# Weight blocks loaded and decoded in pairs, with other waits and ranks in the plan

## The chip, the core and the metric

The kernel runs on one core of one Trainium2 chip. The core has a matrix engine (PE in the profile), a vector engine (DVE), a scalar engine (ACT), a general engine (POOL) and SP, which here only issues transfers to the core's 16 DMA engines. Each engine works through its own instructions in the order in which they were written out, and waits for others by semaphores. The metric is the device time of one execution in microseconds (us), the median of several runs. Lower is better.

## What is computed

Causal attention with a decay bias over 8 batches of 8 heads, 576 positions and head size 64, and behind it a feed-forward layer of 4608 tokens, width 512 and inner width 2048. The weights of the second part come as 64-bit floats.

```python
scores = scale * np.matmul(q, k.transpose(0, 1, 3, 2))
cum = np.cumsum(np.maximum(s, 0.0), axis=-1)
bias = -(cum[:, :, :, None] - cum[:, :, None, :])
scores = np.where(causal, -1000000000.0, scores + np.minimum(bias, 0.0))
attn = np.exp(scores - np.max(scores, axis=-1, keepdims=True))
attn = attn / (np.sum(attn, axis=-1, keepdims=True) + 1e-09)
x = np.matmul(attn, v)            # then tokens x 512
h = x @ w_in                      # 512 -> 2048
g = np.where(h > 0.0, h, np.exp(np.minimum(h, 0.0)) - 1.0)
out = g @ w_out                   # 2048 -> 512
```

## The kernel before

**A plan.** The code does not issue instructions in the order in which it is written. Every piece of work is an operation with a priority, the ways in which it can be done (an engine and an estimated cost for each), and what it reads and writes. `Plan.issue` then picks, again and again, the operation with the smallest rank: the time at which it could start by the plan's estimates, and among those that could start at the same time the smaller priority number. It so writes out one fixed order for each engine. The estimates are nanoseconds; a load costs SP 460 ns and lands when a modelled pipe of 225 bytes per ns has passed its bytes, plus 1800 ns. PE operations that fill gaps (`fillers`, L1547: transposes of an identity that nothing reads) take a rank 350 ns later than their start, and exist only in the first 60 us of planned time.

**Attention.** The first 320 rows of the batches 0 to 2 are done as 12 "low" pairs of heads in 32-bit floats (`prepare_low`, `scoring_low`, `weighing_low`, priorities 0, 10, ... 110). Each pair loads its keys, queries and values, and the row of decay sums: pair (0,1) from the tile `aux` in SBUF, all later ones from the DRAM copy `sums_dram`. `decay_parts` rewrites `aux` in place right after the second pair has been scored. The rest of the attention (`Unit`, priorities from 120) uses 16-bit halves of q, k and v; its operand sets are written to DRAM and read back.

**Feed-forward.** The tokens go in 18 chunks of 256. Chunk 0 is native: it multiplies 32-bit weights (L1423, first layer, into tiles `h`; L1477, second layer, into `o`). The chunks 1 to 17 use weights split in two 16-bit halves, three products for one (L1427 and L1484). Their PE operations have priority 10000 and up: attention goes first where it can start.

**The weights.** `load_unit` handles one block of 128 inner columns (`kind` 0, from w_in) or rows (`kind` 1, from w_out), 128 x 512 values: 32 blocks. Each block is loaded raw (512 KB) into one of four slots of `raws`, and decoded from 64 to 32 bits: one ACT operation (L693), one on DVE or ACT (L697, L699), one on DVE that joins the two into `wa` (L702), and the largest magnitude of the block by DVE (L623) or by ACT (L626, with a second instruction that reads the accumulator). Every load has the sum load of pair (0,1) as a `late` condition: the plan may place it only behind that one's planned landing (`urgent`). When all 32 blocks are there, `weight_scales` finds one scale for each of the two matrices, and `split_unit` splits each block: the high half on POOL, ACT or DVE (L428 to L430), the low half on DVE (L717), with priority -500 + f, ahead of all attention.

**Memory.** `wa` holds 4 tiles of 4 blocks of both kinds (16 KB per partition each), `wp`, the split halves, 4 tiles as large; `raws` shares the first `wp` tile. The values of the first group of units take the place of the last `wp` tile, later ones that of the first `wa` tile; the second operand set takes that of the second `wa` tile, and two of the transposed attention tiles `T` those of the others, once they have been free.

Of the kernel before, what the change touches and what calls it, by code (L numbers as in the profile page):

```python
# [35 lines left out]
LAG, RATE = 1800.0, 225.0  # L36
W0, WD = 25, 3

F_EARLY = 6

W_GROUP = 4

# [5 lines left out]
N_FREE = 0  # L48

N_NATIVE, N_RAW = 1, 4  # L50

FILL_T, GAP = 60e3, 350.0

# [39 lines left out]
class Op:  # L93
    __slots__ = ("ways", "after", "before", "behind", "bufs", "new", "prio", "ready", "left", "filler")


class Plan:
# [97 lines left out]
    def issue(self):  # L195
# [19 lines left out]
        while pending:  # L215
# [11 lines left out]
            for o in pending:  # L227
                t = 0.0
                for b, k in o.new:
# [4 lines left out]
                    if b.others and (b.always or not busy):  # L234
                        for key, bufs, *rule in b.others:
                            if rule and not rule[0](taken[key]):
                                continue
# [6 lines left out]
                else:  # L244
# [9 lines left out]
                    rank = (start + GAP if o.filler else start, o.prio)  # L254
# [4 lines left out]
            if o.filler:  # L259
                start -= GAP  # L260
# [95 lines left out]
def kernel(  # L356
# [223 lines left out]
    NG = NF // W_GROUP  # L580
    w_all = [plan.buf(sb, [P, W_GROUP, 2, 512], F32, f"wa_{g}") for g in range(NG)]
    w_parts = [plan.buf(sb, [P, W_GROUP, 2, 2, 512], F16, f"wp_{g}") for g in range(NG)]

    def weight(f, kind):
        return (w_all[f // W_GROUP], (f, kind)), lambda: w_all[f // W_GROUP].v[:, f % W_GROUP, kind]

    def weight_part(f, kind, part):
        return ((w_parts[f // W_GROUP], (f, kind, part)),
                lambda: w_parts[f // W_GROUP].v[:, f % W_GROUP, kind, part])
# [7 lines left out]
    A_LOW, A_IN, A_OUT = 0, N_LOW * (NP + 1), N_LOW * (NP + 1) + NF + 1  # L597
    A_GROUP = A_OUT + NF + 1
# [38 lines left out]
    def scales_of(prio, spans, dst):  # L637

        n = len(spans)
        kind = int(dst == 0)  # L640
# [25 lines left out]
    def weight_scales():  # L666

        scales_of(-600, [(A_IN, NF + 1), (A_OUT, NF + 1)], 0)
        op(-600, [("DVE-SB", 100.0, lambda: power(
            scales.v.bitcast(U32)[:, 3:4], scales.v.bitcast(U32)[:, 1:2], 2 * 127))],  # L670
           [(scales, 0)], [(scales, 3)])

    urgent = []
    raws = plan.buf(sb, [P, N_RAW, 512, 2], U32, "raws", tag=w_parts[0].key[1])

    def load_unit(f, kind, src):

        prio = W0 + WD * f
        a, n = src.shape[1], f"{'io'[kind]}{f}"
        place, value = weight(f, kind)  # L680
# [972 lines left out]
```

## Time and profile before

| | us |
|---|---|
| median of 3 runs | 1038.81 (1037.28 to 1039.48) |
| the profiled execution | 1034.6 |
| its span, first to last instruction | 1032.8 |
| PE busy | 1003.1 (97%) |
| DVE busy | 845.2 (82%) |
| ACT busy | 669.0 (65%) |
| POOL busy | 295.9 (29%) |

The granted PE clock was 0.996 of full speed over the span. A busy PE counts the fillers too. The view by windows cuts the span into stretches and gives, for each engine, the busy time in it and its number of instructions. The view by lines groups instructions by source line, tile and shape, with the mean time of one in ns and the idle time that the engine had just before them. The timeline lists instructions in order of time, with neighbours of one kind merged; a bracket at the end tells how long the engine sat idle before, and what released it.

### The profile page before, as it was taken

To read this page: it belongs to the slowest core of one execution; us is meant where nothing else is said; L and a number is where in the kernel's file an instruction comes from. 1 tells how busy PE (TensorE), PEld (TensorE's weight loads), DVE (VectorE), ACT (ScalarE), POOL (GpSimd) and SP (SyncE) were. 2 spreads that over 40 slices of the span, in tenths; PEclk is the share of its full clock that TensorE was granted. 3 is DMA by queue.
4 is the path that set the end of the run, shared out by engine and by line. 5 is a ranking of instruction groups with operands and counts; after the bars stand their busy time and mean duration, and the time that the engine had idled before them with its cause. 6 is when DMAs were issued, how large, how long until landed. Compare 5 with 4: busy or idle time off the path is not lost. (4 is left out here: it accounts for less than half of the span.)

```text
span 1032.8 us, 21782 instructions
## 1 busy us (share of the span) xinstructions
PE 1003.1 (97%) x7305; PEld 688.7 (67%) x7305; DVE 845.2 (82%) x2346; ACT 669.0 (65%) x1559; POOL 295.9 (29%) x487
## 2 busy tenths in 40 slices
PE   8889999999999999999999999999999999999998
PEld 6667656676666666666666666676666676666665
DVE  7999998788988988898889999798988898863232
ACT  4898755666667766776776766666675765644343
POOL 6343452242323323241234242222232123100000
PEclk9999999999999999999999999999999999999999
DMA  7997524589979997999989987979998998841000
GB/s 197 276 289 236 150 72 95 124 190 213 222 166 212 207 192 165 198 202 208 196 174 201 232 179 174 229 181 192 215 198 196 227 202 187 182 94 47 1 21 21
DMA packets 296724, 179.83 MB, mean 174 GB/s; under 512 B 209908, under 2 KB 270564, under 8 KB 296612
## 3 DMA queue, kind: packets, MB, share of 16 engines
q1 hardware_dynamic: 296612, 178.45, 75.7%
q8 instruction: 57, 0.93, 0.4%
q14 instruction: 55, 0.45, 0.2%
HBM read 93.08 MB, written 36.81 MB: 126 GB/s over the span
## 5 line engine op out<-in xcount | busy, mean ns | idle before, releaser
L1427 PE MATMUL h<-xh,wp 128*128 128x256 f16 x2176 | 402.7, 273 | 0.7 <-DVE gg L1466 0.7
L1484 PE MATMUL o<-wp,gg 128*128 128x512 f16 x1632 | 392.7, 380 | 0.5 <-DVE gg L1466 0.5
L1427 PEld LDWEIGHTS <-wp 128*128 128x128 f16 x3264 | 317.4, 98 | 69.7 <-issue 2.1
L1427 PE MATMUL h<-xl,wp 128*128 128x256 f16 x1088 | 297.3, 273 | 1.1 <-DVE xl L1403 1.1
L1484 PEld LDWEIGHTS <-gg 128*128 128x128 f16 x1632 | 157.7, 98 | 144.5 <-DVE gg L1466 1.0
L1073 ACT ACTIVATE p<-p,mn 128x192 f32<-128x192 f32 (+1 forms) x232 | 143.7, 620 | 54.9 <-DVE mn L1068 52.9
L1133 DVE SCALAR_TENSOR_TENSOR p<-p,sm,p 128x512 f16<-128x512 f32 (+3 forms) x257 | 162.8, 662 | 4.9 <-POOL p L1125 2.4
L1459 DVE SCALAR_TENSOR_TENSOR h<-g,cs,h 128x512 f32<-128x512 f32 x136 | 102.0, 750 | 60.5 <-ACT g L1446 59.2
L1125 POOL TENSOR_SCALAR p<-p,sm 128x512 f16<-128x512 f32 (+3 forms) x94 | 65.1, 696 | 290.5 <-DVE sm L1079 117.1
L1439 ACT ACTIVATE g<-h,cs 128x512 f32<-128x512 f32 x136 | 92.8, 682 | 78.0 <-PE h L1427 77.2
L1463 ACT ACTIVATE gg<-h 128x512 f16<-128x512 f32 x132 | 78.3, 593 | 83.2 <-DVE h L1459 79.3
L1068 DVE CUSTOM_DVE_ANT_0 p<-sc,maskw 128x192 f32<-128x192 f32 (+1 forms) x232 | 109.5, 481 | 11.9 <-PE sc L1065 8.5
L1065 PE MATMUL sc<-set 128*128 128x288 f16 (+3 forms) x544 | 112.7, 299 | 4.5 <-DVE mn L1068 4.3
L1466 DVE SCALAR_TENSOR_TENSOR gg<-h,gg 128x512 f16<-128x512 f32 x136 | 93.3, 686 | 16.3 <-ACT gg L1463 15.7
L1129 ACT ACTIVATE p<-p,sm 128x512 f16<-128x512 f32 (+3 forms) x139 | 75.1, 557 | 19.0 <-DVE sm L1079 5.5
L1065 PEld LDWEIGHTS <-set 128*128 128x128 f16 x584 | 55.1, 98 | 41.6 <-issue 8.6
L1252 PE MATMUL av<-T,v 128*64 128x256 f16 (+5 forms) x960 | 62.4, 278 | 2.8 <-DMA T<-p 2.8
L1252 PEld LDWEIGHTS <-v 128*64 128x64 f16 x960 | 48.5, 110 | 23.3 <-issue 12.3
L1446 ACT ACTIVATE g<-g 128x512 f32<-128x512 f32 x81 | 50.9, 628 | 1.9
L428 POOL TENSOR_SCALAR v<-va,scales 128x320 f16<-128x320 f32 (+1 forms) x45 | 26.8, 599 | 64.9 <-PE av L1252 58.3
L1073 ACT ACTIVATION_READ_ACCUMULATOR p<-p,mn 128x1 f32 x232 | 43.7, 188 | 0.0
L1068 DVE CUSTOM_DVE_ANT_0 p<-sc,maskw,mn 128x288 f32<-128x288 f32 x64 | 32.9, 514 | 7.1 <-PE sc L1065 5.5
(200 smaller groups left out, 1261.0 us busy)
## 6 DMA issues: line engine op xcount, KB each, us to landing
set<-spread SPq DMA_DIRECT2D x32, 432.0 KB
spread<-parts_None SPq DMA_DIRECT2D x32, 288.0 KB
set<-spread SPq DMA_DIRECT2D x32, 288.0 KB
raws<-in_w_in_dram SPq DMA_DIRECT2D x16, 512.0 KB
raws<-in_w_out_dram SPq DMA_DIRECT2D x16, 512.0 KB
out_dram<-ost SPq DMA_DIRECT2D x32, 256.0 KB
va<-in_vb_dram SPq DMA_DIRECT2D x16, 352.0 KB
xc<-x_dram SPq DMA_DIRECT2D x22, 256.0 KB
```

The costliest lines, as they stand in the source:

```text
L1065: pe_.matmul(view(sc.v[:, :cw]), l, r, start=n == 0, stop=n == len(pairs) - 1)
L1068: op(prio, [("DVE", 84 + dve_p(cw), lambda i=i, sc=sc: dve.tensor_tensor_reduce(pt.v[:, i * cw : (i + 1) * cw], sc.v[:, :cw], mv(i * cw, c ...
L1073: op(prio, [("ACT", 480 + w / 1.2, lambda: act.activation(pt.v[:, :w], pt.v[:, :w], AF.Exp, bias=mn.v[:, n - 1 : n], scale=-1.0, accum_out ...
L1129: ("ACT", 295 + size / 1.2, lambda part=part: act.activation(part(0), own(part), AF.Copy, scale=sm.v[:, r])),
L1133: ("DVE-SB", dve_2(size), lambda part=part: dve.scalar_tensor_tensor(part(1), own(part), sm.v[:, r], part(0), ALU.mult, ALU.subtract)),
L1252: pe_.matmul(av.v[w.h * HB : (w.h + 1) * HB, dst], w.values.v[:, w.h, kb, v], part(w, kb, m), start=kb == 0 and m == 0 and v == 0, stop=kb ...
L1427: pe_.matmul(columns(k), weight_part(f, 0, part)[1]()[:, c * P : (c + 1) * P], xx.v[:, c], start=(c == 0 and m == 0), stop=(c == NCB - 1 a ...
L1439: op(side, [("ACT", act_c(W) + (0 if native else 90), lambda: act.activation(g.v, hp.v, AF.Exp, scale=1.0 if native else by(3)))], [hp] + ...
L1459: op(side, [("DVE", dve_p(W), lambda: dve.scalar_tensor_tensor(hp.v, g.v, by(2 if sign[0] else 1), hp.v, ALU.mult, ALU.max))], [g, cs], [hp])
L1463: ("ACT", act_c(W), lambda: act.activation(gg.v[:, 0], hp.v, AF.Copy, scale=2.0**-DOWN)),
L1466: op(side, [("DVE", dve_p(W), lambda: dve.scalar_tensor_tensor(gg.v[:, 1], hp.v, 2.0**-DOWN, gg.v[:, 0], ALU.mult, ALU.subtract))], [hp, ( ...
L1484: pe_.matmul(acc[i].v, gg.v[:, g, at], weight_part(f, 1, part)[1](), start=(f == 0 and m == 0), stop=(f == NF - 1 and m == 2),)
```

## The change

- The weights are handled in 16 pairs of blocks (128 x 1024 values, 1 MB raw): `load_pair` and `split_pair` in place of `load_unit` and `split_unit`. The raw tiles are four of 1 MB, in the places of the four `wp` tiles of w_out. A pair of w_in is read in rows of 256 columns (2 KB), before 128 (1 KB). The plan counts 5 bytes for a value that has 8.
- The loads of weights have no `late` condition any more. All of batch 0's pairs take their sums from `aux`, and `decay_parts` comes after the fourth pair.
- Each operation has a `gap` that is added to its start in the rank, though not to its start: 400 ns for the weights' loads and decoding, 0 for the splits, 350 for fillers as before. The splits have priority 130 + p.
- The scales of w_in and w_out are found one after the other, and the small operations of a chunk that need only w_in's scale no longer wait for the other's.
- Scores may use the `h` banks until the first `x` tile has been taken, before until the eighth `h`. `wa` and `wp` are tiles of one kind each, and so the tiles that later take their places wait for other blocks: the second operand set for w_in's pairs 3 to 5, the values of later groups for w_in's pairs 0 to 2, two `T` tiles for w_out's pairs 0 to 5.

```diff
-LAG, RATE = 1800.0, 225.0
-W0, WD = 25, 3
-F_EARLY = 6
+LAG, RATE, RAW = 1800.0, 225.0, 5
+W0, WD = 25, 6
+W_PAIRS = 3, 3, 2
-N_FREE = 0
-N_NATIVE, N_RAW = 1, 4
+N_NATIVE, PRIO_SPLIT = 1, 130
+W_GAP, S_GAP = 400.0, 0.0
...
-                    rank = (start + GAP if o.filler else start, o.prio)
+                    rank = (start + o.gap, o.prio)
...
-    w_all = [plan.buf(sb, [P, W_GROUP, 2, 512], F32, f"wa_{g}") for g in range(NG)]
-    w_parts = [plan.buf(sb, [P, W_GROUP, 2, 2, 512], F16, f"wp_{g}") for g in range(NG)]
+    w_all = [plan.buf(sb, [P, n, 2 * 512], F32, f"wa_{kind}_{g}") for kind in range(2) for g, n in enumerate(W_PAIRS)]
+    w_parts = [plan.buf(sb, [P, W_GROUP // 2, 2, 2 * 512], F16, f"wp_{kind}_{g}") for kind in range(2) for g in range(NG)]
...
-    def weight_scales():
-        scales_of(-600, [(A_IN, NF + 1), (A_OUT, NF + 1)], 0)
+    def weight_scales(kind):
+        scales_of(-600, [((A_IN, A_OUT)[kind], NFP + 1)], kind)
...
-    raws = plan.buf(sb, [P, N_RAW, 512, 2], U32, "raws", tag=w_parts[0].key[1])
-    def load_unit(f, kind, src):
-        prio = W0 + WD * f
+    raws = [plan.buf(sb, [P, 2 * 512, 2], U32, f"raw_{g}", tag=w_parts[NG + g].key[1]) for g in range(NG)]
+    def load_pair(p, kind):
+        prio, n = W0 + WD * p, 2 * 512
...
-            slot = (2 * f + kind) % N_RAW
+            slot = raws[(2 * p + kind) % NG]
...
-                 lambda: src.bitcast(U32), [], [(raws, (slot, 0)), (raws, (slot, 1))], P * 4096,
-                 urgent if f >= N_FREE else ())
+                 lambda: src.bitcast(U32), [], [(slot, 0), (slot, 1)], P * n * RAW)
...
-    def split_unit(f, kind):
-        prio, col = -500 + f, slice(kind, kind + 1)
+    def split_pair(p, kind):
+        prio, col = PRIO_SPLIT + p, slice(kind, kind + 1)
...
-            if (b, j) == (0, 1):
-                o = load(prio, lambda: u.k.v[at], lambda: aux.v[h0 : h0 + 2, 0, :LOW],
+            if not b:
+                load(prio, lambda: u.k.v[at], lambda: aux.v[h0 : h0 + 2, 0, :LOW],
...
-            return lambda n: n < last
+            return lambda taken, key: taken[key] < last
...
-                        others=[("h", N_H, opening(1 + N_NATIVE * NFP)), ("o0", 1, opening(1)), ("o1", 1, opening(1))])
+                        others=[("h", N_H, lambda taken, key: not taken[xh.key]), ("o0", 1, opening(1)), ("o1", 1, opening(1))])
...
-                        others=[(w_all[g].key[1], 1, lambda n: n > 0) for g in range(2, NG)], always=True)
+                        others=[(w_all[NW + g].key[1], 1, lambda taken, key: taken[key] > 0) for g in range(2)], always=True)
...
-            if u is todo[1][0]:
+            if u is todo[NP - 1][0]:
                 decay_parts()
...
-        op(side, [("DVE-SB", 600.0, steps)],
-           [(scales, 0), (scales, 3)] + [(scales, c) for c in cols if c > 3], [cs])
+        op(side, [("DVE-SB", 480.0, steps)],
+           [(scales, 0)] + [(scales, c) for c in cols if c > 3], [(cs, "in")])
+        op(side, [("DVE-SB", 120.0, lambda: dve.tensor_scalar(
+            cs.v[:, 4:5], cs.v[:, 3:4], scales.v[:, 3:4], 2.0**DOWN, ALU.mult, ALU.mult))],
+           [(scales, 3), (cs, "in")], [(cs, "out")])
...
-    load_weights(0, F_EARLY)
+    for p in range(NFP):
+        for kind in range(2):
+            plan.gap = W_GAP
+            load_pair(p, kind)
+            plan.gap = 0.0
     xc = load_x(0, chunks[0])
-    load_weights(F_EARLY, NF)
-    weight_scales()
-    for f in range(NF):
-        split_unit(f, 0)
-        split_unit(f, 1)
+    for kind in range(2):
+        weight_scales(kind)
+    for p in range(NFP):
+        for kind in range(2):
+            plan.gap = S_GAP
+            split_pair(p, kind)
+            plan.gap = 0.0
```

More of the change, by code (lines that the diff above doesn't have):

```diff
@@ L93 @@
 class Op:
-    __slots__ = ("ways", "after", "before", "behind", "bufs", "new", "prio", "ready", "left", "filler")
+    __slots__ = ("ways", "after", "before", "behind", "bufs", "new", "prio", "ready", "left", "filler", "gap")
 class Plan:
@@ L235, in issue @@
                         for key, bufs, *rule in b.others:
-                            if rule and not rule[0](taken[key]):
+                            if rule and not rule[0](taken, key):
                                 continue
@@ L258, in issue @@
             (start, _), o, n = best
-            if o.filler:
-                start -= GAP
+            start -= o.gap
             engine, cost, trace = o.ways[n][:3]
@@ L705, in load_unit @@
         else:
             load(prio, lambda: value().rearrange("p (a n) -> p a n", a=a), lambda: src,
-                 [], [place], P * 2048, urgent)
-        peak(prio, 512, value, [place], (A_IN, A_OUT)[kind] + f,
-             aside=(lambda: raw(0).bitcast(F32)) if wide else None, also=[(raws, (slot, 0))] if wide else [])
-    def split_unit(f, kind):
-        prio, col = -500 + f, slice(kind, kind + 1)
-        place, value = weight(f, kind)
-        (high, high_v), (low, low_v) = (weight_part(f, kind, m) for m in range(2))
-        scaled(prio, 512, high_v, value, lambda: scales.v[:, col], [place, (scales, 0)], [high])
-        op(prio, [("DVE-SB", dve_2(512), lambda: dve.scalar_tensor_tensor(
-            low_v(), value(), scales.v[:, col], high_v(), ALU.mult, ALU.subtract))],
-           [place, (scales, 0), high], [low])
@@ L721, in load_weights @@
-    def load_weights(f0, f1):
-        wi = w_in.rearrange("(c p) f -> p c f", p=P)
-        wo = w_out.rearrange("(f p) (a m) -> f p a m", p=P, a=1)
-        for f in range(f0, f1):
-            fs = slice(f * P, (f + 1) * P)
-            load_unit(f, 0, wi[:, :, fs])
-            load_unit(f, 1, wo[f])
+                 [], [place], P * n * 4)
+        peak(prio, n, value, [place], (A_IN, A_OUT)[kind] + p,
+             aside=(lambda: raw(0).bitcast(F32)) if wide else None, also=[(slot, 0)] if wide else [])
@@ new lines, in split_pair @@
+    def split_pair(p, kind):
+        prio, col = PRIO_SPLIT + p, slice(kind, kind + 1)
+        place, value = weight_pair(p, kind)
+        (high, high_v), (low, low_v) = (weight_part(2 * p, kind, m) for m in range(2))
+        scaled(prio, 2 * 512, high_v, value, lambda: scales.v[:, col], [place, (scales, kind)], [high])
+        op(prio, [("DVE-SB", dve_2(2 * 512), lambda: dve.scalar_tensor_tensor(
+            low_v(), value(), scales.v[:, col], high_v(), ALU.mult, ALU.subtract))],
+           [place, (scales, kind), high], [low])
@@ L1042, in prepare @@
              lambda: u.vs.v[:, :1, 0].bitcast(F32), used, [u.vs])
+    xh, xl = (plan.buf(sb, [P, NCB, TMAX], F16, n, tag=n) for n in ("xh", "xl"))
     plan.signal = (id(ps), "o0")
@@ L1332, in attention @@
             step()
-    xh, xl = (plan.buf(sb, [P, NCB, TMAX], F16, n, tag=n) for n in ("xh", "xl"))
     def load_x(ch, rows):
@@ L1517, in output @@
             ]
-            op(side, [w for w in ways if only is None or w[0] in only], reads + [cs], writes)
+            op(side, [w for w in ways if only is None or w[0] in only], reads + [(cs, "out")], writes)
         for i in range(NTB):
```

78 lines of the change are left out of this document (43 added, 35 removed).

## The prediction

> **What bounds the kernel now.** I read the page first, then the view by windows, then the lines, timeline and DMA view of the stretches that the change touches. First the windows: start and end, length, busy time and number of instructions of PE, of the weight loads (PEld), DVE, ACT and POOL, then the granted PE clock, the busy share of the DMA engines and GB/s.
>
> ```profile
> span 1032.8 us, 21782 instructions
> PE 1003.1 (97%) x7305; PEld 688.7 (67%) x7305; DVE 845.2 (82%) x2346; ACT 669.0 (65%) x1559; POOL 295.9 (29%) x487
> ```
> ```profile
> 0.00:20.00 20.00, 14.87 (x92) 13.28 (x92) 14.21 (x33) 8.37 (x27) 14.94 (x38) 0.91 0.65 153
> 20.00:60.00 40.00, 36.69 (x251) 26.41 (x251) 36.08 (x117) 33.44 (x99) 15.49 (x34) 1.00 0.97 291
> 60.00:120.00 60.00, 57.34 (x325) 41.55 (x323) 54.60 (x178) 50.44 (x150) 18.62 (x48) 1.00 0.81 237
> 120.00:150.00 30.00, 29.51 (x110) 18.14 (x110) 29.08 (x77) 17.77 (x35) 16.48 (x17) 1.00 0.24 77
> 150.00:200.00 50.00, 47.48 (x335) 32.46 (x334) 42.91 (x122) 28.65 (x67) 14.69 (x24) 0.97 0.39 93
> 200.00:1000.00 800.00, 788.32 (x6009) 538.20 (x6007) 659.46 (x1810) 519.37 (x1166) 215.68 (x327) 1.00 0.82 179
> ```
> ```profile
> L1547 PE MATMUL scratch<-ident 128*128 128x128 f32 x140 | 19.0, 287 | 0.0
> ```
> ```profile
> L1423 PE MATMUL h<-x,wa x128: 378/380/484, 59.8 to 144.0; 128*128 128x256 f32 x128
> ```
>
> PE is the bound from 60 us on: idle 2.7 us in 60 to 120, 0.5 in 120 to 150, 2.5 in 150 to 200, 11.7 in the next 800. Only the start is different. In the first 60 us PE sits idle 5.1 + 3.3 = 8.4 us, and 19.0 us of its busy time are fillers: 27.4 of 60 us give nothing. This ends where chunk 0's matmuls begin, at 59.8 us; from there PE has spare work. What sets that point is DVE and ACT: in 20 to 60 they are busy 36.1 and 33.4 of 40 us, with the low pairs' softmax and the decoding of weights. So the change is worth what it brings chunk 0's start forward, plus stalls that it removes behind it; PE's own work (1003.1 - 19.0 = 984 us) stays.
>
> **Decoding and splitting, 32 blocks to 16 pairs.** The lines of the stretch from 17 to 119 us, and others that give the price of a width:
>
> ```profile
> L693 ACT ACTIVATE raws<-raws 128x512 f32<-128x512 f32 x32 | 21.6, 678 | 0.6 <-DMA raws<-in_w_in_dram 0.3 <-DMA raws<-in_w_out_dram 0.3
> L626 ACT ACTIVATE raws<-wa 128x512 f32<-128x512 f32 x14 | 9.5, 680 | 1.8 <-DVE wa L702 1.5
> L702 DVE SCALAR_TENSOR_TENSOR wa<-raws 128x512 uint32<-128x512 uint32 x32 | 22.4, 703 | 1.0 <-ACT raws L693 0.3 <-DVE raws L697 0.2
> L697 DVE TENSOR_SCALAR raws<-raws 128x512 uint32<-128x512 uint32 x29 | 13.0, 451 | 0.8 <-DMA raws<-in_w_in_dram 0.8
> L623 DVE TENSOR_REDUCE peaks<-wa 128x1 f32<-128x512 f32 x18 | 12.2, 679 | 0.1
> ```
> ```profile
> L626 ACT ACTIVATION_READ_ACCUMULATOR raws<-wa x14: 178/181/196, 25.2 to 118.9; 128x1 f32 x14
> ```
> ```profile
> L626 ACT ACTIVATE junk<-va 128x704 bf16<-128x704 f32 x4 | 3.2, 789 | 1.5 <-DMA va<-in_vb_dram 1.3
> ```
> ```profile
> L626 ACT ACTIVATE junk<-vs 128x448 bf16<-128x448 f32 x2 | 1.2, 578 | 0.4 <-DMA vs<-in_vb_dram 0.4
> ```
> ```profile
> L623 DVE TENSOR_REDUCE peaks<-vs 128x1 f32<-128x448 f32 x8 | 4.9, 608 | 0.0
> ```
> ```profile
> 34.13 1.23 ACT L693 ACTIVATE raws<-raws 128x512 f32<-128x512 f32 x2
> ```
> ```profile
> 41.75 0.67 DVE L623 TENSOR_REDUCE peaks<-wa 128x1 f32<-128x512 f32 x1
> 42.34 0.60 DVE L623 TENSOR_REDUCE peaks<-vs 128x1 f32<-128x448 f32 x1
> ```
>
> ACT: 704 elements take 789 ns and 448 take 578, so 0.824 ns for one and 0.21 us fixed. DVE: 679 for 512 and 608 for 448 give 1.11 ns and 0.11 us fixed. That is what joining two operations saves at most. Neighbours overlap, though: two of L693 took 1.23 us and not 2 x 0.678, so 0.13 of the fixed part is hidden on ACT and 0.08 counts; on DVE an L623 of 0.67 was followed by the next 0.59 after its start, 0.02 above 512 x 1.11 ns. Joined are on DVE 16 of L702, 14 of L697 and 9 of L623, 39 x 0.02 to 0.11 = 0.8 to 4.3 us; on ACT 16 of L693 and 7 of L626, 23 x 0.08 to 0.21 = 1.8 to 4.8, and 7 accumulator reads at 0.181 = 1.3. In all 3.9 to 10.4 us of engine time, and as the two engines share the softmax and both are nearly full, half of it in time: 2.0 to 5.2. I take the middle, **-3.8**. SP saves 16 issues of about 0.6 us (rows below) that no engine stood waiting for: 0. The splits are joined too, but lie beside native matmuls (L1423 to 144 us, L717 in the fence on the stall below), which hide them: 0; were that cover gone, 16 joined L717 at 0.02 to 0.11 would be 0.3 to 1.8 us more gain.
>
> **Loads that wait for nothing, and sums from SBUF.** SP's issues and PE at the start:
>
> ```profile
> 13.67 0.65 SPq L404 DMA_DIRECT2D kl<-aux  x1
> ...
> 17.55 0.59 SPq L404 DMA_DIRECT2D raws<-in_w_in_dram  x1
> ...
> 20.91 1.28 SPq L404 DMA_DIRECT2D kl<-sums_dram  x2
> ```
> ```profile
> 15.56 1.41 PE L1065 MATMUL sc<-kl,low_queries 128*128 128x128 f32 x4 [3.08 <-issue]
> ...
> 22.53 4.15 PE L1547 MATMUL scratch<-ident 128*128 128x128 f32 x36
> 26.52 0.44 PE L1065 MATMUL sc<-kl,low_queries 128*128 128x128 f32 x2
> ```
>
> The removed wait hardly binds: the first raw load leaves at 17.55 us, 3.9 behind the load of the sums of pair (0,1), and SP's order is kept by that load's own wait for `aux`. DVE and ACT waited 0.8 + 0.6 us for raw data in all (rows above): at most 0.7 in time, I take **-0.3**. What binds is the next pair: (0,2) read its sums back from DRAM at 20.91, and PE turned 36 fillers, 4.15 us, until its scores at 26.52. From `aux` they can be issued behind 13.67. That is worth 0 to 4.1; DVE and ACT filled part of that time with decoding, which now comes later, so I take **-1.5**. `decay_parts` moves off the front with it, same work. The last raw loads are 1 MB and in rows twice as long: no engine waits for them now, 0.
>
> **Order: softmax ahead, splits behind.** PE's one long stall after 60 us, the splits, and the clock behind the stall:
>
> ```profile
> 155.04 0.43 PE L1218 MATMUL tr_None<-ident,psh_None 128*128 128x128 f32 x1 [2.13 <-ACT psh_None L1090]
> ```
> ```profile
> 155.00:159.00 4.00, 3.96 (x21) 0.57 0.52 159
> ```
> ```profile
> 148.09 4.80 DVE L717 SCALAR_TENSOR_TENSOR wp<-wa,scales,wp 128x512 f16<-128x512 f32 x4
> ```
> ```profile
> L717 DVE SCALAR_TENSOR_TENSOR wp<-wa,scales,wp x32: 734/742/1628, 130.0 to 166.5; 128x512 f16<-128x512 f32 x32
> ```
>
> PE waited 2.13 us for the first unit's normalized pair, which stood behind splits on DVE, and then ran 4 us at 0.57 of its clock (columns here: start and end, length, PE busy, clock, DMA), 1.7 us lost: 3.8 together. With the splits behind that unit (priority 130 against 120 and 125) this wait can go; late next are chunk 1's first splits, of which it needs one pair at a time. Range 0 to 3.8, and against it that operations twice as long stand in front of softmax steps; I take a third, **-1.3**. The Trainium skill's page "TensorE: Matmul & The Clock Gate" (Part 1, What's actually happening) says that the clock falls to half only after an idle window of about 3.4 us; here it fell after 2.13 us, so the measurement decides. By the page this term would be a third of 2.1, 0.7.
>
> **Added, and moved for free.** One more chain for a scale:
>
> ```profile
> L650 DVE TENSOR_REDUCE own<-flat 128x1 f32<-128x128 f32 x4 | 1.1, 286 | 0.1
> ```
> Six small DVE operations, none longer than this, at most 1.7 us, beside native matmuls; against the DVE-full stretch 120 to 150 I count **+0.1**. The buffers that change places (second operand set behind pairs 3 to 5 of w_in and their now later splits) can be late by some us where PE has chunk 1 to do: 0; if that cover fails, a PE stall like the one above. The plan behind 200 us is a new one with the same work: its idle 11.7 us can move by some 3 either way; not in the sum.
>
> Sum: -3.8 - 0.3 - 1.5 - 1.3 + 0.1 = **-6.8 us**. The profiled execution took 1034.6 (1.8 around the span of 1032.8) and would be 1027.8; the median of the runs shown lies 4.2 above it, so 1038.8 - 6.8 = 1032.0.
>
> **Rivals.** *DMA ahead of softmax (slower).*
>
> ```profile
> q1 hardware_dynamic: 11928, 16.96, 97.0%
> raws<-in_w_in_dram SPq DMA_DIRECT2D x11, 512.0 KB
> raws<-in_w_out_dram SPq DMA_DIRECT2D x10, 512.0 KB
> ```
> ```profile
> L404 SPq DMA_DIRECT2D x_dram<-xl x12: 320/332/538, 24.3 to 128.1; - x12
> ```
> In 20 to 80 us one queue holds all data, its transfers fill 97% of the engines, and 21 raw loads are 11.0 of its 16.96 MB. Raw tiles for 4.2 MB, where there were 2.1, let twice as much stand ahead of a low pair's queries and values: 14.4 us at 291 GB/s against 7.2. Pairs end every (128.1 - 24.3) / 11 = 9.4 us, and a pair's queries can be loaded one pair ahead; so from a backlog of 9.4 us on the softmax waits. A full one costs 5.0 us and 1.7 of clock, and as DVE and ACT then wait too, joining gains nothing: +6.7, 1045.5. For it: the engines are full already, and a plan that counts 5 bytes for 8 believes less backlog than there is. Against it: waits for raw data are 1.4 us now, though the loads took all that the DMA could give; and the plan's new count is near the trace: 11.0 MB at 8/5 of 225 GB/s and 5.96 at 225 make 30.6 + 26.5 = 57 us where the trace took 60. The Trainium skill's "DMA: Bandwidth & Descriptors" (Queues, rings and completion order) says that each DMA engine consumes the descriptors of one queue in ring order; by that rule this rival needs nothing but the backlog. No row of this profile shows that order.
>
> *Swallowed (no change).* DVE is busy 29.1 of 30 us in 120 to 150. If low pairs and native work end earlier but the splits do not, PE waits there for what it gained: 1038.8. Against it: chunk 1 needs its splits one pair at a time.
>
> *Only the joining.* The new order does nothing that it says, loads and sums go out as before: -3.8 + 0.1, 1035.1.
>
> **Chances.** Forecast 0.48 (own range 1028 to 1035), only joining 0.14, swallowed 0.14, DMA 0.24. About 0.2% (2.1 us) is what a measurement of this kernel can tell from no change: faster 0.62, same 0.14, slower 0.24. The low end takes the upper bounds, 5.2 + 0.7 + 4.1 + 3.8 = 13.8, and 3 of the later plan: 1022; the high end takes the DMA rival: 1046.
>
> **What would show it.** Right: L1423 begins at 53 to 56 us; L702 and L693 x16 at about 1.2 and 1.1 us; fillers well under 19 us; no wait of PE at L1218 near 150 us with a slow clock behind it. Wrong: softmax or score matmuls of the low pairs waiting for loads of `low_queries`, `vs` or `kl` between 20 and 60 us (DMA), or PE idle before L1427 between 140 and 170 (swallowed), or more than 15 us of PE idle behind 200.

## The result, and the profile after

| | before | after |
|---|---|---|
| median, runs side by side | 1037.1 (1034.1 to 1039.5) | 1042.9 (1042.1 to 1046.7) |
| ratio | | 1.0062, interval 1.0044 to 1.0080 |
| the profiled execution | 1034.6 | 1042.1 |
| chunk 0's first matmul, us | 59.8 | 66.4 |
| chunk 1's first matmul, us | 151.8 | 161.7 |
| PE idle in 200 to 1000 us | 11.7 | 2.8 |

The changed kernel is 0.6% slower; 0.7% faster was forecast, with this time inside the wide range. The page of the changed kernel, its windows (columns as in the prediction), its fillers and the rows of chunk 0 and chunk 1; the last row is chunk 1 of the kernel before:

```profile
span 1040.3 us, 21651 instructions
PE 1009.4 (97%) x7314; PEld 691.3 (66%) x7314; DVE 826.9 (79%) x2281; ACT 679.3 (65%) x1543; POOL 272.0 (26%) x476
```
```profile
0.00:20.00 20.00, 16.82 (x104) 14.14 (x104) 13.25 (x32) 8.74 (x28) 15.16 (x40) 1.00 0.61 154
20.00:60.00 40.00, 31.34 (x204) 24.24 (x202) 27.14 (x82) 28.27 (x72) 12.16 (x29) 0.91 0.90 289
60.00:120.00 60.00, 56.81 (x342) 38.27 (x341) 49.08 (x183) 47.90 (x134) 21.43 (x60) 1.00 0.61 186
120.00:150.00 30.00, 28.00 (x117) 18.14 (x116) 25.70 (x71) 21.59 (x38) 5.12 (x9) 1.00 0.87 240
150.00:200.00 50.00, 42.86 (x249) 27.96 (x248) 47.05 (x112) 38.35 (x75) 16.49 (x25) 0.93 0.54 134
200.00:1000.00 800.00, 797.22 (x6071) 545.41 (x6069) 652.86 (x1788) 519.90 (x1176) 201.66 (x314) 1.00 0.79 174
```
```profile
L1549 PE MATMUL scratch<-ident 128*128 128x128 f32 x145 | 21.8, 308 | 0.0
```
```profile
L1425 PE MATMUL h<-x,wa x128: 379/379/483, 66.4 to 158.0; 128*128 128x256 f32 x128
L1429 PE MATMUL h<-xh,wp x2176: 269/273/287, 161.7 to 1029.0; 128*128 128x256 f16 x198
```
```profile
L1427 PE MATMUL h<-xh,wp x2176: 270/273/422, 151.8 to 1021.5; 128*128 128x256 f16 x198
```

PE's busy time up to 200 us, less the fillers, was 185.9 - 19.0 = 166.9 us before and is 175.8 - 21.8 = 154.0 now: 12.9 us of work fall behind. Of these 797.2 - 788.3 = 8.9 us are made up in the next 800, where PE now hardly idles, and 4.0 are not. That is not the whole loss of 7.5 us between the two spans. Over the whole span PE idles about as long as before (30.9 us against 29.7) and has 2.8 us more of fillers; the other 3.5 us are PE's own work, which keeps it busy 987.6 us in place of 984.1. The mean granted clock was 0.993 against 0.996, which over such a span makes 3 us: it stood at 0.61 in 28 to 32 us, and below 0.9 in 52 to 60.

DVE and ACT, which set the start before (36.1 and 33.4 of 40 us busy in 20 to 60), are busy only 27.1 and 28.3 there: they wait too. For what, the loads on SP and the use of a pair's values by DVE (the reduction that finds their peak) show. The timeline of before, SP's loads of `vs` and stores of finished pairs, then DVE's use of the first two:

```profile
23.00 0.52 SPq L404 DMA_DIRECT2D vs<-in_vb_dram  x1
...
37.59 0.33 SPq L404 DMA_DIRECT2D x_dram<-xl  x1
...
45.92 0.41 SPq L404 DMA_DIRECT2D x_dram<-xl  x1
```
```profile
29.15 0.61 DVE L623 TENSOR_REDUCE peaks<-vs 128x1 f32<-128x448 f32 x1
42.34 0.60 DVE L623 TENSOR_REDUCE peaks<-vs 128x1 f32<-128x448 f32 x1
```

The same of the changed kernel, with the raw loads that leave first, PE's scores that wait for queries, and a last fence of DVE's waits up to 120 us (sum, times, longest):

```profile
17.42 0.59 SPq L403 DMA_DIRECT2D raw<-in_w_in_dram  x1
18.05 1.48 SPq L403 DMA_DIRECT2D raw<-in_w_out_dram  x1
19.57 0.47 SPq L403 DMA_DIRECT2D raw<-in_w_in_dram  x1
20.09 0.57 SPq L403 DMA_DIRECT2D raw<-in_w_out_dram  x1
...
22.12 0.76 SPq L403 DMA_DIRECT2D vs<-in_vb_dram  x1
...
44.71 0.86 SPq L403 DMA_DIRECT2D x_dram<-xl  x1
...
54.96 0.41 SPq L403 DMA_DIRECT2D x_dram<-xl  x1
```
```profile
34.85 0.61 DVE L630 TENSOR_REDUCE peaks<-vs 128x1 f32<-128x448 f32 x1
53.55 0.62 DVE L630 TENSOR_REDUCE peaks<-vs 128x1 f32<-128x448 f32 x1 [2.13 <-DMA vs<-in_vb_dram]
```
```profile
34.14 0.79 PE L1066 MATMUL sc<-kl,low_queries 128*128 128x128 f32 x4 [1.48 <-DMA low_queries<-in_qT_dram]
```
```profile
DVE peaks L630 <- DMA vs<-in_vb_dram: 6.3, 5, 2.1
DVE peaks L630 <- DMA va<-in_vb_dram: 3.8, 2, 3.5
```

Four raw loads of 1 MB leave between 17.42 and 20.09 us, at the same moment as four of half a MB did before (17.55 to 20.30). The values of the next pair, asked for 2 us later, are used 12.7 us after their issue (22.12 to 34.85), before 6.1 (23.00 to 29.15). In the last fence 10.1 us of DVE's waits go to `vs` and `va`; before, DVE waited for neither. The second low pair ends 7.1 us later, the third 9.0. Chunk 0's first matmul itself waits for nothing in either kernel: PE comes to it from the score matmul in front without a gap, so that its start is the place that the plan gave it, moved by what the instructions ahead waited for.

### The profile page after: what moved, and what is told of

Read it like the earlier page. It is cut to its first block, busy times and chain, and to the rows that moved or that the text cites. A ratio compares the mean times of both kernels' runs of the same rounds, so it can differ in the third digit from the quotient of the medians.

```text
span 1040.3 us, 21651 instructions
## 1 busy us (share of the span) xinstructions
PE 1009.4 (97%) x7314; PEld 691.3 (66%) x7314; DVE 826.9 (79%) x2281; ACT 679.3 (65%) x1543; POOL 272.0 (26%) x476
## 5 line engine op out<-in xcount | busy, mean ns | idle before, releaser
L1429 PE MATMUL h<-xh,wp 128*128 128x256 f16 x2176 | 397.0, 273 | 0.0
L1134 DVE SCALAR_TENSOR_TENSOR p<-p,sm,p 128x512 f16<-128x512 f32 (+3 forms) x251 | 153.3, 640 | 4.7 <-ACT p L1130 2.6
L1461 DVE SCALAR_TENSOR_TENSOR h<-g,cs,h 128x512 f32<-128x512 f32 x136 | 102.1, 751 | 68.7 <-ACT g L1448 66.4
L1126 POOL TENSOR_SCALAR p<-p,sm 128x64 f16<-128x64 f32 (+3 forms) x98 | 66.4, 682 | 243.4 <-DVE sm L1080 88.1
L1066 PE MATMUL sc<-set 128*128 128x288 f16 (+3 forms) x544 | 110.5, 298 | 1.6 <-DVE mn L1069 0.7
L1130 ACT ACTIVATE p<-p,sm 128x64 f16<-128x64 f32 (+3 forms) x139 | 73.2, 545 | 22.9 <-issue 5.2
L1066 PE MATMUL sc<-kl,low_queries 128*128 128x192 f32 (+2 forms) x110 | 31.1, 385 | 9.1 <-DVE mn L1069 4.4
```

Source lines behind the costliest of these rows:

```text
L1066: pe_.matmul(view(sc.v[:, :cw]), l, r, start=n == 0, stop=n == len(pairs) - 1)
L1130: ("ACT", 295 + size / 1.2, lambda part=part: act.activation(part(0), own(part), AF.Copy, scale=sm.v[:, r])),
L1134: ("DVE-SB", dve_2(size), lambda part=part: dve.scalar_tensor_tensor(part(1), own(part), sm.v[:, r], part(0), ALU.mult, ALU.subtract)),
L1429: pe_.matmul(columns(k), weight_part(f, 0, part)[1]()[:, (2 * c + k) * P :][:, :P], xx.v[:, c], start=(c == 0 and m == 0), stop=(c == NCB ...
L1461: op(side, [("DVE", dve_p(W), lambda: dve.scalar_tensor_tensor(hp.v, g.v, by(2 if sign[0] else 1), hp.v, ALU.mult, ALU.max))], [g, (cs, "i ...
```

## The experiments

Ratios are to the kernel before, run side by side on the same chip, with 95% intervals. "Low pair n ends" is the n-th store `x_dram<-xl`; "the last decode" is the start of the last operation that joins into `wa`. Each profile is of one execution.

### One part of the changed kernel taken back

**a_two_slots**: two raw tiles in place of four, so 2.1 MB can stand in the queue, as before.

```diff
-    raws = [plan.buf(sb, [P, 2 * 512, 2], U32, f"raw_{g}", tag=w_parts[NG + g].key[1]) for g in range(NG)]
+    raws = [plan.buf(sb, [P, 2 * 512, 2], U32, f"raw_{g}", tag=w_parts[NG + g].key[1]) for g in range(2)]
...
-            slot = raws[(2 * p + kind) % NG]
+            slot = raws[(2 * p + kind) % 2]
```


> The changed kernel with two raw tiles of 1 MB in place of four, so that 2.1 MB and not 4.2 of weights can stand in the one DMA queue ahead of a low pair's loads; all else as changed. Theory 1 (backlog: the low pairs wait for loads behind the weights): the first native matmul comes back from 66.4 us to 60 or before, PE waits no more for low_queries (3.3 us in the changed kernel) and DVE less than 3 us for vs (6.3), and the time is about 6 us below the changed kernel, near 1037, ratio to before 1.000. Theory 2 (order: the gap of 400 ns puts decoding behind softmax, so that the last block is decoded at 168 us instead of 118 and chunk 1 starts late): first native matmul may move, but the last decoding stays behind 160 us and chunk 1 behind 160, ratio 1.005 or more.

1056.0 us, 1.0173 (1.0141 to 1.0204). The values of the next pair are used at 28.84 us, 8.0 after their issue at 20.87; low pairs 2 to 4 end at 41.4, 46.7 and 52.1 (44.7, 55.0, 60.2 in the changed kernel; 37.6, 45.9, 53.8 before). The backlog is gone, and with it the lateness of the low pairs 3 and 4. But the time gets worse: chunk 0 begins at 69.8 us, the last decode comes at 169.7, and PE waits for decoded weights, as theory 2 said. Its waits from 60 to 210 us:

```profile
PE o L1479 <- DVE wa L711: 8.5, 1, 8.5
PE o L1479 <- DVE gg L1457: 6.9, 5, 2.1
PE h L1425 <- DVE wa L711: 3.1, 1, 3.1
```

So something else in the change holds decoding back; with four tiles PE had none of these waits.

**a_gap0**: no handicap for loads and decoding.

```diff
-W_GAP, S_GAP = 400.0, 0.0
+W_GAP, S_GAP = 0.0, 0.0
```


> The changed kernel with a gap of 0 for the weights' loads and decoding (400 ns as changed). Theory 2 (order): the last decoding ends by 130 us (168 as changed), chunk 1's first matmul starts by 155 us (161.7), its second layer by 170 (188.4), PE's clock in 150 to 200 is back over 0.96 (0.93), and the time is 5 to 9 us below the changed kernel, ratio to before 0.997 to 1.001. Theory 1 (backlog): the start is as late as in the changed kernel or later, first native matmul at 66 us or behind it, and the ratio stays at 1.004 or more.

1043.2 us, 1.0057 (1.0040 to 1.0075): the time of the changed kernel, by another road. The last decode comes at 97 us (168.5 with the gap), but now the raw loads, which wait for nothing, leave at 6.74 us ahead of the first pair, which ends at 35.6 in place of 25.4. Chunk 0 begins at 73.4 us, chunk 1 at 179.0. Theory 2 was right about the decoding, and wrong about chunk 1 and the time.

**a_raw8**: the plan counts the true 8 bytes.

```diff
-LAG, RATE, RAW = 1800.0, 225.0, 5
+LAG, RATE, RAW = 1800.0, 225.0, 8
```


> The changed kernel with the true 8 bytes a value in the plan's pipe in place of 5. If the plan's optimism about loads is the cause, waits for loads of low_queries, vs and raw go and the time falls by 4 us or more below the changed kernel. Theory 1 in its plain form (the loads are issued all the same and stand ahead) and theory 2 expect a change of less than 3 us either way: first native matmul at 62 to 70 us, last decoding behind 150 us.

1052.4 us, 1.0143 (1.0114 to 1.0171). The low pairs 2 and 3 end at 53.2 and 67.9, later still, chunk 0 begins at 82.1, and PE stands 8.0 us before a scale's transposition (`flat`) whose peaks are not there. No theory had such a loss.

**a_split_first**: the splits' old priority.

```diff
-N_NATIVE, PRIO_SPLIT = 1, 130
+N_NATIVE, PRIO_SPLIT = 1, -500
```


> The changed kernel with the splits ahead of all attention again (priority -500 in place of 130). If the splits' place is what starves PE between 160 and 200 us, PE is busy over 47 of 50 us in 150 to 200 (42.9 as changed) and the time falls by 3 us or more. Theory 2 puts the delay into the decoding and the scale of w_out (187 us), ahead of the splits: then the last decoding stays behind 160 us and the time within 2 us of the changed kernel. Theory 1 expects no difference before 140 us.

1042.7 us, 1.0051 (1.0030 to 1.0072). The order of instructions is the same on every engine as in the changed kernel: a priority decides only between operations that could start at the same time, and here there was no such case. What it measures is how well things repeat: the time well (1.0051 against 1.0062), single points of one execution less so (chunk 0 begins at 67.5 in place of 66.4, low pair 2 ends at 47.5 in place of 44.7).

### Parts put into the kernel before

**b_gap400**: the gap for weights alone, with single blocks (shown without the lines that give each operation its gap).

```diff
+            plan.gap = 400.0
             load_unit(f, 0, wi[:, :, fs])
             load_unit(f, 1, wo[f])
+            plan.gap = 0.0
```


> The kernel before with one part alone: a gap of 400 ns for loading and decoding of the weights, in blocks of 512 KB and with the late condition. Theory 2 (the gap lets all softmax go ahead, decoding comes last, and the native chunk and the splits wait for it): low pairs end earlier (the twelfth by 115 us, 128 before), the last decoding behind 145 us (117.6 before), PE idle or clocked down for 6 us or more between 60 and 200, ratio 1.003 to 1.015. Theory 1 expects nothing from the gap: ratio 0.998 to 1.002.

1055.2 us, 1.0189 (1.0172 to 1.0206). The low pairs do go ahead (pairs 3 to 5 end at 43.2, 50.3 and 55.2, 2.7 to 8.1 us earlier), but the last decode comes at 169.2 us (117.6 before), and chunk 0, which begins at 79.8, runs dry. PE's waits from 60 to 210 us:

```profile
PE h L1425 <- DVE wa L702: 12.3, 2, 7.5
PE o L1479 <- DVE gg L1457: 7.5, 4, 2.1
```

**b_aux**: the sums of all of batch 0 from `aux`.

```diff
-            if (b, j) == (0, 1):
+            if not b:
...
-            if u is todo[1][0]:
+            if u is todo[NP - 1][0]:
```


> The kernel before with one part alone: sums of all of batch 0 from aux, decay_parts behind the fourth pair. The prediction's term for it was -1.5 us (0 to -4.1): pair (0,2)'s scores before 26.5 us, 0.996 to 1.000. If the early gain is a rearrangement that DVE and ACT give back, ratio 1.000 to 1.003.

1033.7 us, 0.9991 (0.9974 to 1.0008). The scores of pair (0,2) begin at 22.06 us in place of 26.52, and yet no time is won for this pair, the third: low pair 2 ends at 40.5 (37.6), low pair 3 at 47.8 (45.9). The total does not move by what can be measured.

### The joined operations in the old order

**pairs_only**: the changed kernel with all of its order taken back: the loads' wait, no gap, two raw tiles (the same 2.1 MB as before), 8 bytes, splits at -500.

```diff
-LAG, RATE, RAW = 1800.0, 225.0, 5
+LAG, RATE, RAW = 1800.0, 225.0, 8
-N_NATIVE, PRIO_SPLIT = 1, 130
+N_NATIVE, PRIO_SPLIT = 1, -500
-W_GAP, S_GAP = 400.0, 0.0
+W_GAP, S_GAP = 0.0, 0.0
...
-    raws = [plan.buf(sb, [P, 2 * 512, 2], U32, f"raw_{g}", tag=w_parts[NG + g].key[1]) for g in range(NG)]
+    raws = [plan.buf(sb, [P, 2 * 512, 2], U32, f"raw_{g}", tag=w_parts[NG + g].key[1]) for g in range(2)]
...
-            slot = raws[(2 * p + kind) % NG]
+            slot = raws[(2 * p + kind) % 2]
...
-                 lambda: src.bitcast(U32), [], [(slot, 0), (slot, 1)], P * n * RAW)
+                 lambda: src.bitcast(U32), [], [(slot, 0), (slot, 1)], P * n * RAW, urgent)
...
+                if j == 1:
+                    urgent.append(o)
```


> The changed kernel with the order of before put back: late condition on the weights' loads, gap 0, two raw tiles (2.1 MB), 8 bytes counted, splits at -500. What is left of the change: weights in pairs, sums of batch 0 from aux, scales by kind, memory. If the loss lies in the order and the backlog (theories 1 and 2 together), this is as fast as before or faster by up to 4 us, ratio 0.996 to 1.001, first native matmul at 55 to 61 us. If the joined operations or the memory's new places cost by themselves (theory 3: an operation twice as long stands in front of a softmax step, a raw tile of 1 MB comes free only as a whole), ratio 1.003 or more and first native matmul behind 62 us.

1031.1 us, 0.9950 (0.9922 to 0.9977): faster than both. `vs` is used 6.1 us after its issue again (22.39 to 28.50), and chunk 0 begins at 58.2 us, chunk 1 at 159.0:

```profile
L1428 PE MATMUL h<-x,wa x128: 379/379/483, 58.2 to 149.3; 128*128 128x256 f32 x128
```

Two things here stand against a simple account. Low pairs 2 to 4 end at 44.2, 52.7 and 57.0, nearly as late as in the changed kernel, although there is no backlog; what makes them late here stays open. And chunk 1 begins 7.2 us later than in the kernel before, while the time is 5.4 us shorter.

Decoding costs DVE and ACT 71.5 us in place of 83.3 (the groups of `raw`, `wa` and their peaks up to 210 us; in the changed kernel they make 73.9); two of its rows, to be set beside L702 and L693 of before:

```profile
L712 DVE SCALAR_TENSOR_TENSOR wa<-raw 128x1024 uint32<-128x1024 uint32 x16 | 19.7, 1232 | 1.4 <-ACT raw L703 1.1
L703 ACT ACTIVATE raw<-raw 128x1024 f32<-128x1024 f32 x16 | 18.5, 1162 | 4.1 <-DMA raw<-in_w_in_dram 4.1
```

**a_late_gap0**: the wait and gap 0 alone; four tiles, 5 bytes and priority 130 stay.

```diff
-W_GAP, S_GAP = 400.0, 0.0
+W_GAP, S_GAP = 0.0, 0.0
...
-                 lambda: src.bitcast(U32), [], [(slot, 0), (slot, 1)], P * n * RAW)
+                 lambda: src.bitcast(U32), [], [(slot, 0), (slot, 1)], P * n * RAW, urgent)
...
+                if j == 1:
+                    urgent.append(o)
```


> The changed kernel with gap 0 and the late condition put back, four raw tiles, 5 bytes. Against the run with gap 0 alone, whose raw loads left at 6.7 us and whose first low pair ended at 35.6, the first raw load leaves again behind 13 us. Theory 1 (backlog ahead of the low pairs): the first pair ends by 26 us, the second by 46, the first native matmul starts 5 us or more before that run's 73.4, and the ratio is at most 1.003. If the wait is worth nothing: first native matmul at 70 us or behind it, ratio 1.004 or more.

1054.3 us, 1.0185 (1.0166 to 1.0204). Chunk 0 does come 9.6 us earlier than without the wait, at 63.8, and 2.6 earlier than in the changed kernel, but the time is far from the 1.003 that was to follow. Low pairs 2 and 3 end at 47.3 and 54.4; the last decode comes at 95.8, low pair 12 ends only at 144.1, and chunk 1 begins at 179.8. No single wait is long here (4.0 us at most by kind in 60 to 120), so the cause stays open. The five runs that follow put the parts of the new order into pairs_only one at a time.

**p_gap400**, the gap:

```diff
-W_GAP, S_GAP = 0.0, 0.0
+W_GAP, S_GAP = 400.0, 0.0
```

> The joined kernel in the old order (two raw tiles, loads behind the sums of pair (0,1), 8 bytes, splits at -500: 1031.1 us) with the gap of 400 on all weight loads and decoding alone. Theory 'the gap starves the chunk': decoding goes behind all softmax, the last decode moves from 144 to 165 us or later, chunk 1 begins behind 170 instead of 159, and the time is 1045 to 1052 (the gap alone cost the kernel before 19 us). Rival 'the queue of raw loads': with two raw tiles no backlog can form, so the time stays at 1029 to 1034.

1046.6 us, 1.0092 (1.0074 to 1.0110). The last decode moves from 144.2 to 165.3 us, chunk 1 from 159.0 to 177.2, and two kinds of waits in 60 to 210 us make 17.7 us:

```profile
PE o L1482 <- DVE gg L1460: 12.3, 4, 5.7
PE h L1428 <- DVE wa L712: 5.4, 2, 2.8
```

The expected signs came, and the picture is that of b_gap400: with the gap alone PE waits for decoding.

**p_four**, the deeper queue:

```diff
-    raws = [plan.buf(sb, [P, 2 * 512, 2], U32, f"raw_{g}", tag=w_parts[NG + g].key[1]) for g in range(2)]
+    raws = [plan.buf(sb, [P, 2 * 512, 2], U32, f"raw_{g}", tag=w_parts[NG + g].key[1]) for g in range(NG)]
...
-            slot = raws[(2 * p + kind) % 2]
+            slot = raws[(2 * p + kind) % NG]
```

> The joined kernel in the old order with four raw tiles instead of two and nothing else. Theory 'the queue of raw loads': 4.2 MB of raw data stand ahead of the queries and values of low pairs 2 to 4, which end 5 to 10 us later than 44.2, 52.7 and 57.0; chunk 0 begins at 63 to 68 instead of 58.2 and the time is 1036 to 1042. Rival 'the gap': without it, more raw tiles cost nothing, 1029 to 1033.

1058.6 us, 1.0207 (1.0191 to 1.0223), 17 us above the upper end of what was expected; chunk 0 begins at 71.5. `vs` is used at 36.05 us, 14.2 after its issue at 21.81, and low pairs 2 to 4 end at 46.4, 59.6 and 77.9 (44.2, 52.7 and 57.0 with two tiles). With the data late, PE stands twice at an instruction that the plan had placed for earlier data:

```profile
60.66 0.80 PE L665 MATMUL flat<-ident,tops 128*128 128x128 f32 x2 [4.79 <-DVE tops L654]
...
101.13 0.77 PE L665 MATMUL flat<-ident,tops 128*128 128x128 f32 x2 [4.33 <-DVE tops L654]
```

**p_split130**, the splits' new priority:

```diff
-N_NATIVE, PRIO_SPLIT = 1, -500
+N_NATIVE, PRIO_SPLIT = 1, 130
```

> The joined kernel in the old order with the splits at priority 130 in place of -500 and nothing else. If the priority of the splits is innocent (it was, undone alone in the changed kernel: 1.0051 against 1.0062): 1029 to 1034, chunk 1 begins at 157 to 162. If the splits, put behind native work and softmax, come late for chunk 1: it begins behind 165 and the time is 1036 to 1045.

1036.4 us, 0.9997 (0.9982 to 1.0012), 5 us above pairs_only, chunk 1 at 159.4: the time of the second case with the sign of the first.

**p_raw5**, the plan's count of bytes:

```diff
-LAG, RATE, RAW = 1800.0, 225.0, 8
+LAG, RATE, RAW = 1800.0, 225.0, 5
```

> The joined kernel in the old order, with 5 bytes counted for 8 in the plan's data rate and nothing else. With two raw tiles the loads are held by the tiles and not by the count: 1029 to 1034. If a load that the plan believes shorter makes it place weight loads ahead of the low pairs' loads: pairs 2 to 4 end 3 us or more later, 1035 to 1040. A difference with neither sign would be the scatter of plans with the same work.

1068.4 us, 1.0309 (1.0286 to 1.0332), the worst of all, and not for the reason that was expected: pairs 2 to 4 end earlier than in pairs_only (43.2, 48.4, 55.9). The timeline of DVE, then of PE:

```profile
122.04 13.76 DVE L727 SCALAR_TENSOR_TENSOR wp<-wa,scales,wp 128x1024 f16<-128x1024 f32 x10
135.72 0.16 DVE L1082 TENSOR_SCALAR sml<-sml 128x5 f32<-128x5 f32 x1
```
```profile
136.63 0.47 PE L844 MATMUL trl<-ident,pl 128*128 128x128 f32 x1 [15.36 <-POOL pl L1090]
```

Here the splits, with priority -500, go out as one block on DVE, with a softmax step of 0.16 us behind them, and PE waits 15.4 us for what follows from it. The other 22 us are not accounted for. In the changed kernel the way back from 5 bytes to 8 costs time too (a_raw8), so this constant has no price of its own: either value, put in alone, gave a worse plan.

**p_nolate**, no wait of the loads:

```diff
-                 lambda: src.bitcast(U32), [], [(slot, 0), (slot, 1)], P * n * RAW, urgent)
+                 lambda: src.bitcast(U32), [], [(slot, 0), (slot, 1)], P * n * RAW)
```

> The joined kernel in the old order without the loads' wait for the sums of pair (0,1), nothing else. The wait hardly bound in the kernel before (a first raw load at 17.55 us, 3.9 behind that load), but without a gap the raw loads could go out from 7 us on, ahead of the low pairs, as they did in the changed kernel without the gap (first low pair ended at 35.6 instead of 25.4): then the first pair ends behind 30 us and the time is 1036 to 1045. If the two tiles hold them: 1029 to 1034.

1037.4 us, 0.9996 (0.9974 to 1.0018). The first pair ends at 28.8 in place of 23.7: the raw loads do go ahead, less than the first case said (behind 30), and the time lies in its range.

### Controls: edits without a purpose

Single parts put into pairs_only cost up to 37 us, the whole new order 12; that asks for a control. One assumption of the plan, the rate of its modelled pipe, is altered by 0.4%; the work is the same, its order another on every engine.

```diff
-LAG, RATE = 1800.0, 225.0
+LAG, RATE = 1800.0, 226.0
```


> Control: the kernel before, with the data rate that the plan assumes 226 in place of 225, nothing else. Theory 'each part has its price': an edit without a purpose moves nothing, within 3 us of 1037. Rival 'scatter of plans': the planner lays out another order of the same work and the time moves by 5 us or more, most likely upward, as the order before is a chosen one.

> Control: the changed kernel, with an assumed rate of 226 in place of 225, nothing else. 'Each part has its price': 1040 to 1046. 'Scatter of plans': 5 us or more away from 1042.9, most likely upward, 1048 to 1070.

> Control: the joined kernel in the old order, with an assumed rate of 226 in place of 225, nothing else. 'Each part has its price': 1028 to 1034. 'Scatter of plans': 1037 or more; then what four raw tiles, the 5 bytes and the gap cost when put in singly is no price of theirs.

> Third layout of the kernel before: an assumed rate of 224. Theory 'the change has a price': with 1036.6 and 1029.5 it stays under 1038, chunk 0 begins by 62 us and low pairs 2 and 3 end by 40 and 50 us. Rival 'scatter alone': 1025 to 1055, overlapping the changed kernel's 1042.9 and 1039.0.

> Third layout of the changed kernel: an assumed rate of 224. Theory 'the change has a price': 1038 or more, chunk 0 begins at 66 us or later and low pairs 2 and 3 end behind 42 and 52 us, whatever the layout. Rival 'scatter alone': 1025 to 1055, with a fair chance under 1036.

| assumed rate | before | after | pairs_only |
|---|---|---|---|
| 224 (d_) | 0.9952 (0.9932 to 0.9971) | 0.9991 (0.9972 to 1.0011) | |
| 225 | 1 | 1.0062 (1.0044 to 1.0080) | 0.9950 (0.9922 to 0.9977) |
| 226 (c_) | 0.9934 (0.9908 to 0.9960) | 1.0031 (1.0019 to 1.0043) | 0.9965 (0.9949 to 0.9980) |
| mean | 0.9962 | 1.0028 | 0.9958 |

The kernel before and pairs_only were expected to lose by such an edit, as chosen orders; the one gained 7.1 us, the other lost 1.6 by the ratios, whose intervals overlap. c_after, at 1039.0, lies between its two cases. d_before came as the first theory had it; d_after kept the late chunk 0 and low pairs of that theory, but at 1035.8 not its time. An edit without a purpose moves the time by up to 0.7%, as much as the change did. The means over three layouts, before and after, lie 0.66% apart (6.8 us), but with a scatter of about 0.35% in each column that difference is uncertain by some 0.3% (one standard error), and the columns overlap: 1 before, 0.9991 after. The kernel before at 226 is the fastest run of the study, 1029.5 us, faster than both kernels compared. The starts of chunk 0 and chunk 1 separate the two kernels better than the time does. Before at 226 and 224, then after at 226 and 224:

```profile
L1423 PE MATMUL h<-x,wa x128: 379/379/462, 60.3 to 146.0; 128*128 128x256 f32 x128
L1427 PE MATMUL h<-xh,wp x2176: 269/273/286, 149.6 to 1017.1; 128*128 128x256 f16 x198
```
```profile
L1423 PE MATMUL h<-x,wa x128: 379/379/634, 61.0 to 148.5; 128*128 128x256 f32 x128
L1427 PE MATMUL h<-xh,wp x2176: 269/273/287, 152.1 to 1016.4; 128*128 128x256 f16 x198
```
```profile
L1425 PE MATMUL h<-x,wa x128: 379/379/483, 67.8 to 155.4; 128*128 128x256 f32 x128
L1429 PE MATMUL h<-xh,wp x2176: 269/273/287, 159.1 to 1025.3; 128*128 128x256 f16 x198
```
```profile
L1425 PE MATMUL h<-x,wa x128: 378/379/483, 73.6 to 157.3; 128*128 128x256 f32 x128
L1429 PE MATMUL h<-xh,wp x2176: 269/273/418, 165.1 to 1025.9; 128*128 128x256 f16 x198
```

With the two at 225, chunk 0 begins at 59.8 to 61.0 before and at 66.4 to 73.6 after, chunk 1 at 149.6 to 152.1 and at 159.1 to 165.1. Low pair 2 ends at 36.6 to 37.6 and at 44.6 to 46.2. These do not overlap, and a_split_first, the same order as after, lies with the after ones or beyond. But the layout of after in which chunk 0 and chunk 1 come last, at 224, is the fastest of its three: by how much a late chunk 0 lengthens the time is not to be read off here.

## Why the prediction was wrong

**The bound was read rightly, its link to the time too simply.** PE has spare work from chunk 0 on: its idle time in 200 to 1000 us fell from 11.7 to 2.8. Chunk 0 was to begin at 53 to 56 us with well under 19 us of fillers; it began at 66.4, with 21.8. In all three layouts both starts are later than in any of before. But the time does not simply follow them: a_late_gap0 begins chunk 0 earlier than the changed kernel and is slower, pairs_only begins chunk 1 later than before and is faster.

**The step that failed: loads and order costed as small gains.** "Loads that wait for nothing" stood at -0.3 us and "softmax ahead, splits behind" at -1.3, and the doubled raw tiles had a price only in a rival. In the changed kernel the removed wait brought the first raw load forward by 0.13 us (17.55 to 17.42), so it was indeed nothing there; the doubled tiles and the gap were not nothing, and with them a start forecast 4 to 7 us earlier came 6.6 us later.

- *The backlog.* The mechanism of the rival "DMA ahead of softmax", given a chance of 0.24, is what the trace shows: its sign, a low pair waiting for `low_queries` and `vs` between 20 and 60 us, is there. That its price of 6.7 us comes near the 5.8 measured is luck as far as these runs go, since the 5.8 hold the gap and the scatter of plans as well. Two tiles brought the use of `vs` from 12.7 us behind its issue to 8.0; four tiles in pairs_only moved it from 6.1 to 14.2, and low pairs 2 to 4 end 2, 7 and 21 us later. The argument against this rival was that engines waited only 1.4 us for raw data; it looked at the wrong waits. What a backlog delays is the small loads behind it, and of those the trace of before had none that was late.
- *The gap.* No rival covered it. The prediction took "softmax may go ahead" as a gain of up to 3.8 us and asked only what stands in front of softmax. It did not ask who waits for the decoding that is put behind: chunk 0 itself, which needs a pair of blocks of each matrix at a time. Alone the gap costs 18.9 parts in a thousand in the kernel before and 14 in pairs_only (0.9950 to 1.0092), nearly all of it seen as PE's waits for `wa` and for the `gg` behind it. In the changed kernel itself PE has no such wait from 60 to 210 us. There the late decoding (last decode at 168.5 us, 117.6 before) shows further on: 7.0 us of waits for a scale (`flat`, `every`) and for split tokens and weights (`xl`, `wp`), of which the kernel before had none.

Taking one of the two back (a_two_slots, a_gap0) gains nothing. That the deep queue and the gap partly mend each other would explain it, but is an inference. How the 5.8 us divide between them, and how much of it is scatter, is not to be had from these runs.

**Joining.** The operations came out as costed (1.23 us on DVE, 1.16 on ACT for 1024 elements), and the saving in engine time near the top of the 3.9 to 10.4 us given: 83.3 - 73.9 = 9.4 in the changed kernel, 83.3 - 71.5 = 11.8 in pairs_only. (The middle of 2.0 to 5.2 is 3.6 and not 3.8; the sum would be -6.6, which changes nothing else.) Whether half of it reaches the time is not shown: pairs_only gains 5.4 us on the one layout, but the means of the table, 0.9958 and 0.9962, are the same within their scatter.

**Sums from SBUF.** The step was right and its worth is unproven. The row of pair (0,2)'s scores moved from 26.52 us to 20.47; b_aux, which does this alone, is within its interval of no change. In the changed kernel the next scores, those of the fourth pair, then wait until 34.14 us for their queries; what takes the time back in b_aux stays open.

**The stall by the splits.** It was not removed. PE still waits for the normalized pair (at 184.57 us, 1.19 us), and the clock still falls behind it and two more waits, which is the last section's case. Priority 130 for -500 changed nothing in the changed kernel's order; p_raw5, with priority -500, shows the stall in another layout, 15.4 us long.

**"Swallowed".** Part of it came too: in 150 to 200 us PE idles 7.1 us, where it was 2.5, mostly in waits for `xl`, for splits and for the normalized pair, as the splits begin only at 150.9 us.

**The plan behind 200 us.** "Some 3 us either way" was too small. The idle time there fell by 8.9, and the controls put whole runs 0.2 to 0.7% apart with no change of work. A chance for "within 0.2%" has little meaning when any edit redraws the plan: range and chances should have had this term first.

## What to carry to other kernels

When a planner writes the order, first measure two or three edits without a purpose; only a difference beyond their scatter, or one that shows at the same place in every layout (here the start of chunk 0), belongs to the change. Such a place need not be what sets the time: check that the time follows it. Deeper prefetch is not free on a full queue: ask which small load stands behind it and who waits for that. An operation that is told to let others go first needs the same question as one that is put in front: who waits for its result.

## What the runs showed of the hardware

**A load is late by what was issued ahead of it in its queue.** The first `vs` that is issued behind raw loads is used 6.1 to 9.0 us after its issue in the twelve runs with 2.1 MB of raw data ahead (before and pairs_only 6.1, p_nolate 9.0), and 11.8 to 14.2 us in the eight with 4.2 MB (c_after 11.8, p_four 14.2). The means, 7.4 and 13.2, lie 5.7 us apart; 2.1 MB take 7.3 us at the 289 GB/s of that stretch. A use is the latest moment at which the data can have landed; in c_after, p_nolate and others the engine did wait for it. The rule of the Trainium skill's "DMA: Bandwidth & Descriptors" (Queues, rings and completion order), that descriptors of one queue are consumed in ring order, which no row of the kernel before could show, agrees with this.

**The clock fell without any long wait.** PE's windows of the changed kernel, and the waits that come before them in two answers of the timeline:

```profile
164.00:168.00 4.00, 3.38 (x29) 2.66 (x28) 3.86 (x12) 0.09 (x1) 1.56 (x2) 1.00 0.16 39
...
184.00:188.00 4.00, 1.95 (x13) 1.27 (x14) 3.70 (x16) 2.01 (x5) 2.43 (x7) 1.00 0.77 163
188.00:192.00 4.00, 2.02 (x7) 0.38 (x5) 4.00 (x9) 4.00 (x5) 0.34 (x1) 0.52 1.12 168
```
```profile
163.61 0.27 PE L1429 MATMUL h<-xl,wp 128*128 128x256 f16 x1 [1.65 <-DVE xl L1405]
```
```profile
184.57 0.33 PE L1219 MATMUL tr_None<-ident,psh_None 128*128 128x128 f32 x1 [1.19 <-POOL psh_None L1087]
186.25 0.38 PE L668 MATMUL every<-own,all_ones 128*128 128x1 f32 x2 [0.87 <-DVE own L661]
187.11 0.90 PE L1066 MATMUL sc<-set 128*128 128x192 f16 x4 [0.47 <-DVE pc_None L1152]
```

Three waits of 1.19, 0.87 and 0.47 us within four were followed by a clock of 0.52: it was still full at 188.0 us, and fell before the next wait, of 1.79 us up to 190.73. A single wait of 1.65 at 163.6 us left it at 1.00 in the window behind it. The idle window of about 3.4 us that the Trainium skill's "TensorE: Matmul & The Clock Gate" (Part 1, What's actually happening) names was not there as one unbroken stretch. In this one execution short waits that lie close together were enough.
